# A planned kernel of attention, gated mixture and Fourier mixing: new costs for the list schedule, a new search, nine weight pairs early

## The chip, the cores and the metric

The kernel runs on one core of one Trainium2 chip. A core has five engines with instruction queues of their own: TensorE (PE) for matmuls, VectorE (DVE), ScalarE (ACT), GpSimd (POOL), and SyncE (SP), which only issues DMAs here. They meet by semaphores. The metric is the device time of one launch in microseconds (us), the median over the runs.

## The reference

Attention with a decay, whose output goes through a gated feed-forward layer with a convolution over the sequence, and then through a Fourier-mixing block. B = 4, H = 8, S = 576, D = 64, so that the hidden width is 512.

```
def _attn_ref(q, k, v, f):
    scores = scale * np.matmul(q, k.transpose(0, 1, 3, 2))
    cum = np.cumsum(np.log(np.clip(f, 0.0001, 1.0)), axis=-1)
    decay = cum[:, :, :, None] - cum[:, :, None, :]
    scores = np.where(causal, -1000000000.0, scores + decay)
    scores = scores - np.max(scores, axis=-1, keepdims=True)
    attn = np.exp(scores)
    attn = attn / (np.sum(attn, axis=-1, keepdims=True) + 1e-09)
    return np.matmul(attn, v)

def _moe_ref(x, w_in, conv_w, w_out):              # widths 512, 1024, 512
    h = np.maximum(x @ w_in, 0.0)
    conv_out = sum of conv_w[k] * (h shifted by k - 1), k = 0..2
    return h * sigmoid(conv_out) @ w_out

def _moe2_ref(x, w_ch1, w_ch2):                    # widths 512, 2048, 512
    u = x + real(fft(fft(x, axis=1), axis=2))
    un = (u - mean(u)) / sqrt(var(u) + 1e-06)
    return u + np.maximum(un @ w_ch1, 0.0) @ w_ch2
```

## The kernel before

The whole program is first recorded, then ordered by a planner, then emitted. Every call on an engine (`V.` for DVE, `A.` for ACT, `G.` for POOL, matmuls and transposes for PE, `dma` for SP) makes an operation with a cost from `cost_of`; `analyse` finds which operation must wait for which through the tiles that they touch; `graph` adds to each such pair a time lag from the table `LAG`, by the two engines. `forward` is a list schedule: it lets each engine take, of the operations that are ready by then, the one of least priority number, and charges its cost; it knows a clock of PE that halves a matmul's speed when the last tick had too little PE work, and a lock between DVE and POOL. `backward` runs the same from the end and gives new priorities, `ROUNDS` times over. Then each operation's priority is moved by a letter of the long string `SHIFT`, one letter for each operation, from -32 to +31 us, and a last `forward` gives the order in which everything is emitted:

```
    def order(self):
        self.graph()
        prio = [o.prio for o in self.ops]
        for _ in range(ROUNDS):
            self.forward(prio)
            prio = self.backward()
        for i, c in enumerate("".join(SHIFT.split())):
            prio[i] += 1e3 * (LETTERS.index(c) - 32)
        self.span, out = self.forward(prio)
        return out
```

On the chip the engines run that order, each in its own row, and wait by semaphores; the planner's times are not used. Since one helper emits all operations, the line in the trace is L601 for nearly all of them (L593 for groups of matmuls, L599 for fills); the names of the tiles tell what an instruction is. In the order of the changed kernel these lines are L604, L596 and L602, and the buffer numbers of the names differ by a few (psatt_u__166 for psatt_u__169).

The stages, as far as they are needed:

- **Attention**, 16 pairs of heads (0 to some 250 us). A pair's scores come as 16 and then 8 products into four PSUM tiles `psatt_s`, from `att_qk` (one buffer for the odd pairs, 70, one for the even, 91). DVE reduces each tile into `att_t` and a running minimum `att_nb` (the trace's CUSTOM_DVE_ANT_0, the order's ISA), ACT takes the exponential. The weights are then transposed on PE, 128 x 128 at a time and in groups of three or four, into two PSUM tiles `psatt_u`, and evacuated into `att_pt`: of a pair's eight groups the first two by DVE (512 wide), the next two half by ACT and half by DVE (256 each), the rest by ACT (512 and 384). These groups run about two pairs behind the scores. Then follow the products with the values (`att_tv`), also into `psatt_u`, and two multiplications on DVE into `att_xr`.
- **First feed-forward layer**, beside it and up to some 450 us with the Fourier transform (`psdft`): products into two PSUM tiles `psbc_bc`, `glu_t` and `glu_cv` for the convolution and the gate, with SCALAR_TENSOR_TENSOR of 576 on DVE and TENSOR_TENSOR of 576 on POOL.
- **Fourier block's two products** w_ch1 and w_ch2, 450 us to the end, dense on PE.
- **Weights** come as 64-bit floats and are decoded, 512 columns at a time, in the buffers `wprep_dr` (raw), `wprep_dw`, `wprep_de`: an ACT Abs (ACTIVATE `wprep_dw<-wprep_dr`), a POOL clamp (TENSOR_SCALAR), on DVE a TENSOR_SCALAR and two SCALAR_TENSOR_TENSOR. The tiles of w_out are also folded (a sum of 255 columns on POOL, a difference of 255 on DVE, an ACT copy `wprep_dr<-wprep_de`). `NST` pairs of tiles (one of w_ch1, one of w_ch2) of the 16 are decoded in the attention stage and stored in DRAM; the others late, by `decode_some`.

The functions that the change touches, and their callers:

## Time and profile before

| | |
|---|---|
| median of 3 runs | 857.21 us (856.75 to 858.38) |
| the profiled execution | 855.14 us, its span 853.4 us |
| PE busy | 821.7 us, 96% |
| DVE busy | 651.7 us, 76% |
| ACT busy | 432.8 us, 51% |
| POOL busy | 250.1 us, 29% |
| granted clock of PE, mean | 0.994 |

The span runs from the first to the last instruction; 1.7 us of the execution lie outside it. A row of the timeline gives an instruction's start, its length, its engine, what it writes and reads, and in brackets how long the engine had been idle before it and what it waited for. A matmul's row is longer than the time to the next one's start, since matmuls overlap; the starts tell the pace. The clock is given as a share of 2.4 GHz: 1.00, or 0.50 for 1.2 GHz.

### The profile page before, as it was taken

What the parts mean: (1) busy time and instruction counts of PE and PEld (TensorE: products, weight loads), DVE (VectorE), ACT (ScalarE), POOL (GpSimd) and SP (SyncE); (2) the same over time, 40 slices, a digit from 0 to 9 for tenths busy, and PEclk for the clock granted to TensorE, in tenths of its full rate; (3) what the DMA queues carried; (4) which work ended last, traced back from release to release, by engine and by line L of the source; (5) the groups of instructions that cost most, each with busy time, mean ns of one, the idle gap of its engine ahead of it and who ended that gap; (6) DMA issues with size and microseconds to landing.
All of it is one profiled execution on the core that took longest, in us unless ns stands there. A gap on an engine that the chain in (4) does not pass through costs nothing.

```text
span 853.4 us, 15323 instructions
## 1 busy us (share of the span) xinstructions
PE 821.7 (96%) x5424; PEld 710.6 (83%) x5424; DVE 651.7 (76%) x1596; ACT 432.8 (51%) x1043; POOL 250.1 (29%) x271
## 2 busy tenths in 40 slices
PE   8989998999999999999999999999999999999997
PEld 6657876789888998998888788888889889888896
DVE  6969998875996484269598869879877799867754
ACT  6968887854875384256435344335424453213220
POOL 2244445500451142148747441122113220000000
PEclk9989999999999999999999999999999999999999
DMA  6555464888338634686998744543552835332312
GB/s 225 156 167 176 142 208 133 262 271 269 106 123 283 196 114 145 206 250 175 261 249 199 166 132 99 186 124 101 180 175 82 214 102 154 94 124 63 99 51 86
DMA packets 97804, 139.61 MB, mean 164 GB/s; under 512 B 17048, under 2 KB 59832, under 8 KB 97728
## 3 DMA queue, kind: packets, MB, share of 16 engines
q1 hardware_dynamic: 97152, 135.69, 53.6%
q0 software_dynamic: 576, 2.95, 1.1%
q8 instruction: 42, 0.69, 0.3%
q14 instruction: 34, 0.28, 0.1%
HBM read 105.99 MB, written 35.04 MB: 165 GB/s over the span
## 4 chain that ended last, share of the span: by engine, by line
PE 70%; DVE 13%; ACT 8%; POOL 4%; issue 3%; DMA 2%; SPq 0%; DVEq 0%; ACTq 0%; POOLq 0%
PE psc_c__4743 L601 10%; PE psc_c__4742 L601 10%; PE psbc_bc__554 L601 8%; PE psbc_bc__555 L601 7%; PE psdft_x__3934 L601 5%; PE psdft_x__3935 L601 4%; PE psc_c__5054 L601 4%; PE psc_c__5053 L601 4%; PE psc_c__5051 L601 3%; PE psc_c__5052 L601 3%; PE psatt_u__174 L593 2%; DVE glu_cv__158 L601 2%; DVE glu_cv__157 L601 2%; PE psatt_s__170 L593 2%; PE psatt_u__174 L601 2%
## 5 line engine op out<-in xcount | busy, mean ns | idle before, releaser
L601 ACT ACTIVATE bc_xs__131<-ml_t__5380 128x320 fp32r<-128x320 f32 (+1 forms) x78 | 34.9, 449 | 99.6 <-DVE ml_t__5380 L601 86.6
L601 PE MATMUL psbc_bc__554<-bc_xs__131,bc_wi__130 128*128 128x288 f32 x384 | 68.3, 304 | 2.7 <-ACT glu_t__138 L601 2.2
L601 PE MATMUL psbc_bc__555<-bc_xs__131,bc_wi__130 128*128 128x288 f32 x384 | 67.2, 304 | 0.3 <-ACT glu_t__139 L601 0.3
L601 PEld LDWEIGHTS psbc_bc__554<-bc_xs__131,bc_wi__130 128*128 128x128 f32 x384 | 55.6, 189 | 5.1 <-ACT glu_t__138 L601 2.9
L601 DVE TENSOR_TENSOR ml_t__5380<-psc_c__4742,ml_t__5380 128x320 f32<-128x320 f32 (+1 forms) x91 | 40.8, 459 | 23.5 <-PE psc_c__4742 L601 22.1
L601 PEld LDWEIGHTS psbc_bc__555<-bc_xs__131,bc_wi__130 128*128 128x128 f32 x384 | 55.7, 190 | 1.2 <-ACT glu_t__139 L601 0.5
L601 DVE TENSOR_TENSOR ml_t__5380<-psc_c__4743,ml_t__5380 128x320 f32<-128x320 f32 (+1 forms) x91 | 40.6, 459 | 15.9 <-PE psc_c__4743 L601 14.0
L601 POOL TENSOR_SCALAR wprep_dw__125<-wprep_dw__125 128x512 f32<-128x512 f32 x24 | 18.5, 771 | 114.6 <-ACT wprep_dw__125 L601 114.6
L601 DVE SCALAR_TENSOR_TENSOR bc_xs__131<-ml_t__5380,bc_xs__131 128x320 fp32r<-128x320 f32 (+1 forms) x78 | 38.3, 495 | 11.8 <-ACT bc_xs__131 L601 11.0
L601 DVE SCALAR_TENSOR_TENSOR glu_cv__157<-glu_t__138,bc_cw__132,glu_cv__157 128x576 f32<-128x576 f32 x32 | 32.3, 1009 | 11.2 <-ACT glu_cv__157 L601 10.9
L601 DVE SCALAR_TENSOR_TENSOR glu_cv__158<-glu_t__139,bc_cw__132,glu_cv__158 128x576 f32<-128x576 f32 x32 | 32.6, 1018 | 4.6 <-ACT glu_cv__158 L601 4.3
L601 POOL TENSOR_SCALAR wprep_dw__122<-wprep_dw__122 128x512 f32<-128x512 f32 x24 | 17.9, 746 | 56.6 <-ACT wprep_dw__122 L601 56.6
L601 ACT ACTIVATE ml_t__5382<-ml_t__5380 128x320 fp32r<-128x320 f32 (+1 forms) x26 | 11.7, 449 | 37.9 <-DVE ml_t__5380 L601 37.6
L593 PE MATMUL psatt_s__171<-att_t__67,att_t__66 64*128 64x288 f32 (+2 forms) x48 | 25.4, 530 | 0.0
L593 PE MATMUL psatt_s__170<-att_t__67,att_t__66 64*128 64x288 f32 (+2 forms) x48 | 25.4, 529 | 0.0
L601 DVE COPY glu_t__140<-psbc_bc__555 128x256 f32<-128x256 f32 (+2 forms) x48 | 10.0, 258 | 19.5 <-PE psbc_bc__555 L601 19.5
L593 PE MATMUL psatt_u__174<-att_pt__101,att_tv__92 128*64 128x448 f32 (+3 forms) x80 | 24.0, 452 | 0.4 <-ACT att_pt__102 L601 0.4
L593 PE MATMUL psatt_u__174<-att_pt__102,att_tv__93 128*64 128x448 f32 (+3 forms) x80 | 24.0, 452 | 0.0
L601 ACT ACTIVATE glu_t__140<-psbc_bc__554 128x256 f32<-128x256 f32 (+2 forms) x48 | 8.6, 249 | 25.8 <-PE psbc_bc__554 L601 16.6
L593 PE MATMUL psatt_s__173<-att_t__67,att_t__66 64*128 64x288 f32 (+2 forms) x48 | 20.9, 442 | 0.0
L593 PE MATMUL psatt_s__172<-att_t__67,att_t__66 64*128 64x288 f32 (+2 forms) x48 | 20.8, 439 | 0.0
L593 PE MATMUL psatt_u__169<-att_pt__101,att_tv__99 128*64 128x448 f32 (+4 forms) x72 | 19.3, 413 | 1.2 <-ACT att_pt__102 L601 1.2
(895 smaller groups left out, 2984.5 us busy)
## 6 DMA issues: line engine op xcount, KB each, us to landing
wprep_dr__124<-in_moe_w_ch_dram SPq DMA_DIRECT2D x16, 512.0 KB
wprep_dr__121<-in_moe_w_ch_dram SPq DMA_DIRECT2D x16, 512.0 KB
bc_wo__133<-dram_t__334 SPq DMA_DIRECT2D x13, 512.0 KB
bc_wo__134<-dram_t__334 SPq DMA_DIRECT2D x13, 512.0 KB
att_qk__70<-in_qk_dram SPq DMA_DIRECT2D x8, 608.0 KB
att_qk__91<-in_qk_dram SPq DMA_DIRECT2D x8, 608.0 KB
att_rb__68<-dram_t__333 SPq DMA_DIRECT2D x32, 144.0 KB
dram_t__340<-mr_us__4770 SPq DMA_DIRECT2D x18, 256.0 KB
```

Of the source, the lines that this page charges most:

```text
L593: getattr(eng[op.eng], f)(**{k: v.real() if isinstance(v, View) else v for k, v in kw.items()})
L601: getattr(eng[op.eng], op.fn)(**kw)
```

## The change

Six edits, and all of them act on the order alone, except the first:

- `NST` is 9 instead of 8: one more pair of tiles of w_ch1 and w_ch2 is decoded and stored in the attention stage (34 decodes of 512 there, 32 before; 14 late instead of 16). The number of instructions on each engine and their shapes stay the same.
- `ROUNDS` 17 instead of 53, and a new string `SHIFT` with a new letter for nearly every operation.
- `LAG`: from ACT and DVE to PE 160 and 135 ns instead of 275 and 250, and other, smaller changes.
- `cost_of`: new costs of transposes, Abs, scans, DVE's transposes and POOL's operations; the fixed surcharge for DVE operations within SBUF goes.
- The lock: an operation of DVE (four kinds without PSUM) and one of POOL (two kinds) now delay each other both ways, by what is left of the other one less 90 ns. Before, only DVE paid, 0.8 of the rest of a POOL `tensor_tensor`.
- PE counts as slow when the tick before held under 2500 of work, 3060 before.

```diff
-NWO, NST = 2, 8
+NWO, NST = 2, 9
...
-ROUNDS = 53
+ROUNDS = 17
...
-BSSSSzeZSZ89LigeKBR0aZhwnRmwGp--4-+6++mq-s06+-F-8-6u-alusvgW+66w8ulcpbqmiXV+RBCsuVT+UXRzudhlCz99-BsL23wSPSJBIX
+zKThh1797sjlR+1-h3lY-7e37-pBVDcR9K0--w4ttttowXB0sv7BU0rjUYPCNZSRoYPDmfRXSTDB98-fZiBB3XUwhs--bBBBDBvdBBqjGYuaBQ
...
-       "ACT": {"ACT": 153.0, "DVE": 152.0, "PE": 275.0, "POOL": 170.0, "SP": 135.0},
-       "DVE": {"ACT": 128.0, "DVE": 127.0, "PE": 250.0, "POOL": 155.0, "SP": 120.0},
-       "POOL": {"ACT": 75.0, "DVE": 75.0, "PE": 300.0, "POOL": 102.0, "SP": 67.0},
+       "ACT": {"ACT": 153.0, "DVE": 152.0, "PE": 160.0, "POOL": 190.0, "SP": 135.0},
+       "DVE": {"ACT": 120.0, "DVE": 127.0, "PE": 135.0, "POOL": 190.0, "SP": 120.0},
+       "POOL": {"ACT": 110.0, "DVE": 115.0, "PE": 300.0, "POOL": 102.0, "SP": 105.0},
...
-        return (n * 2 if fn == "transpose" else n * 4 if kw["rhs"].dtype == F32 else max(n, 256)) / 2.4 + 12.0
+        if fn == "transpose":
+            return n * 2 / 2.4 + 2.0
+        if kw["rhs"].dtype == F32:
+            return n * 4 / 2.4 + 12.0
+        return max(n, 256) / 2.4 + (12.0 if n < 400 else 15.0)
...
-        if n > 32 and fn != "memset" and not psum and space.get("out") != "PSUM":
-            c = 1.25 * c + 60.0
         return c
     if fn == "tensor_scalar":
-        return n * 0.833 + 244.0
+        return n * 0.91 + 148.0
...
-def two_reads(fn, kw):
-
-    v = [x for x in kw.values() if isinstance(x, View)]
-    if fn in ("memset", "reciprocal") or "PSUM" in [x.t.slot.pool.space for x in v]:
+def two_reads(eng, fn, kw):
+
+    if eng == "POOL":
+        return fn in ("tensor_tensor", "tensor_scalar")
+    if eng != "DVE" or fn not in ("tensor_tensor", "scalar_tensor_tensor", "tensor_scalar", "tensor_copy"):
         return False
-    return max(x.free() for x in v) > 32
+    return "PSUM" not in [x.t.slot.pool.space for x in kw.values() if isinstance(x, View)]
...
-                if busy.get(tick - 1, 0) < 3060:
+                if busy.get(tick - 1, 0) < 2500:
...
-            if o.eng == "POOL" and o.fn == "tensor_tensor":
-                port.append((t, t + o.took))
-            elif o.pair:
-                o.took = (o.cost - 60.0) / 1.25
-                for a, b in port[-8:]:
-                    if a <= t < b:
-                        o.took += (b - t) * 0.8
-                        break
+            if o.pair:
+                k = o.eng == "POOL"
+                o.took += max(port[1 - k] - 90.0 - t, 0.0)
+                port[k] = t + o.took
```

What this does to the order, at three places. The first is DVE's row at the start, where the first pair's scores are reduced. Before:

```order
L601 SCALAR_TENSOR_TENSOR att_t_0__67<-att_rb__68,att_t_0__67 32x576 x2
L601 TENSOR_SCALAR wprep_de__126<-wprep_dw__125 128x512
L601 ISA att_t_0__75,att_nb__95<-psatt_s__170,att_t_0__65 128x288
L601 ISA att_nb__95 128x1
L601 ISA att_t_0__72,att_nb__95<-psatt_s__170,att_t_0__65 128x192
```

And now:

```order
L604 SCALAR_TENSOR_TENSOR att_t_0__67<-att_rb__68,att_t_0__67 32x576 x2
L604 ISA att_t_0__75,att_nb__95<-psatt_s__167,att_t_0__65 128x288
...
L604 ISA att_t_0__71,att_nb__95<-psatt_s__169,att_t_0__65 128x64
L604 ISA att_nb__95 128x1
L604 ISA att_t_0__76,att_nb__96<-psatt_s__170,att_t_0__65 128x64
L604 ISA att_nb__96 128x1
L604 TENSOR_SCALAR wprep_de__126<-wprep_dw__125 128x512
```

The decode's first step on DVE went from ahead of the eight reduces to behind them.

The second is ACT's row where the eighth pair's weights are evacuated (`att_pt`) and a w_out tile is prepared (`wprep_dr__121<-wprep_de__123`). Before:

```order
L601 ACTIVATE att_pt_0__101<-psatt_u__174 128x2x128
L601 ACTIVATE att_pt_0__102<-psatt_u__169 128x2x128
L601 ACTIVATE bc_xs__131<-att_xr__69 128x576
L601 ACTIVATE wprep_dr__121<-wprep_de__123 128x4x128
L601 ACTIVATE att_pt_0__101<-psatt_u__174 128x4x128
L601 ACTIVATE att_t_0__87,att_sum__103<-att_t_0__87,att_nb__105 128x192
L601 ACTIVATE att_pt_0__102<-psatt_u__169 128x4x128
```

And now:

```order
L604 ACTIVATE att_pt_0__101<-psatt_u__171 128x4x128
L604 ACTIVATE bc_xs__131<-att_xr__69 128x576
L604 ACTIVATE att_pt_0__102<-psatt_u__166 128x4x128
L604 ACTIVATE att_pt_0__101<-psatt_u__171 128x3x128
...
L604 ACTIVATE att_pt_0__102<-psatt_u__166 128x3x128
L604 ACTIVATE att_rt__98<-psatt_u__171 10x128
...
L604 ACTIVATE att_t_0__89,att_sum__103<-att_t_0__89,att_nb__105 128x448
L604 ACTIVATE wprep_dr__121<-wprep_de__123 128x4x128
```

The copy of the w_out tile stands behind the pair's last evacuation, where it stood ahead of four of them. A like exchange is found in the third pair: before, ACT's row has an evacuation `att_pt_0__101<-psatt_u__169 128x2x128`, the Abs `wprep_dw__122<-wprep_dr__121`, and the evacuation `att_pt_0__102<-psatt_u__174 128x2x128`; now both evacuations stand ahead of the Abs.

The third is PE's row behind the first 16 score products of the twelfth pair, where the tenth pair's weights are transposed (`psatt_u<-const`). Before:

```order
L593 MATMUL psatt_s__173<-att_t_0__67,att_t_0__66 128x64
L601 MATMUL psbc_bc__555<-glu_t_0__145,bc_wo__134 128x288
...
L601 MATMUL psatt_u__174<-const_t_0__61,att_t_0__85 128x128 x4
L601 MATMUL psbc_bc__555<-glu_t_0__145,bc_wo__134 128x288
...
L601 MATMUL psbc_bc__555<-glu_t_0__156,bc_wo__134 128x288
L601 MATMUL psatt_u__174<-const_t_0__61,att_t_0__82 128x128
L601 MATMUL psbc_bc__554<-glu_t_0__141,bc_wo__133 128x288
L601 MATMUL psatt_u__174<-const_t_0__61,att_t_0__82 128x128
```

And now:

```order
L596 MATMUL psatt_s__170<-att_t_0__67,att_t_0__66 128x64
L604 MATMUL psatt_u__171<-const_t_0__61,att_t_0__85 128x128 x4
L604 MATMUL psatt_u__166<-const_t_0__61,att_t_0__90 128x128 x4
L604 MATMUL psatt_u__171<-const_t_0__61,att_t_0__82 128x128 x2
...
L604 MATMUL psatt_u__171<-const_t_0__61,att_t_0__84 128x128 x4
L604 MATMUL psatt_u__166<-const_t_0__61,att_t_0__89 128x128 x4
L604 MATMUL psatt_u__171<-const_t_0__61,att_t_0__83 128x128 x3
L596 MATMUL psatt_s__167<-att_qk__91 128x448
```

The products of the feed-forward layer (`psbc_bc`) that stood between the groups are gone from there; 27 transposes stand in a row, with the twelfth pair's last eight score products directly behind. On DVE the order at this place is: copy of 512, a reciprocal of 10 columns, copy of 512, two reduces of 288, copy of 256, a reduce of 192, copy of 256.

At the end of the program the last four steps on DVE are the same in both orders (two additions of 256 from one PSUM bank, one of 512, two of 256 from the other bank). On PE the last three matmuls of 512 stand behind the end of the first bank before, the last ten now.

## Rows read from the trace of the kernel before

**Rows 1.** The page: busy time of each engine, share of the span, instructions.

```profile
PE 821.7 (96%) x5424; PEld 710.6 (83%) x5424; DVE 651.7 (76%) x1596; ACT 432.8 (51%) x1043; POOL 250.1 (29%) x271
```

**Rows 2.** Windows: stretch, length, busy PE, PEld, DVE, ACT, POOL (instructions), PE clock, DMA share, GB/s.

```profile
0.00:62.00 62.00, 54.04 (x368) 36.99 (x370) 47.77 (x173) 46.21 (x136) 18.60 (x40) 0.94 0.58 183
62.00:250.00 188.00, 178.20 (x1398) 150.39 (x1395) 159.96 (x413) 137.06 (x359) 74.97 (x62) 0.99 0.59 188
250.00:450.00 200.00, 192.85 (x1457) 176.35 (x1456) 131.06 (x286) 104.91 (x256) 82.92 (x84) 1.00 0.71 207
450.00:845.00 395.00, 392.73 (x2191) 344.23 (x2191) 309.72 (x721) 144.22 (x293) 73.64 (x86) 1.00 0.45 128
845.00:853.40 8.40, 3.87 (x17) 2.63 (x15) 3.16 (x7) 0.42 (x1) 0.00 (x0) 0.99 0.35 109
```

**Rows 3.** Windows around the two stretches with a lower granted clock.

```profile
51.00:54.40 3.40, 1.54 (x11) 1.15 (x11) 2.45 (x6) 2.05 (x6) 0.61 (x1) 1.00 0.23 57
54.40:61.30 6.90, 6.20 (x28) 2.80 (x28) 3.48 (x13) 5.08 (x16) 2.54 (x2) 0.51 0.36 108
143.20:146.60 3.40, 3.40 (x15) 2.98 (x15) 1.76 (x9) 3.39 (x9) 2.74 (x2) 0.50 0.41 140
```

**Rows 4.** Timeline of POOL, DVE and PE at the first scores.

```profile
10.39 0.61 POOL L601 TENSOR_SCALAR wprep_dw__125<-wprep_dw__125 128x512 f32<-128x512 f32 x1 [7.95 <-ACT wprep_dw__125 L601]
11.04 0.43 DVE L601 TENSOR_SCALAR wprep_de__126<-wprep_dw__125 128x512 int32<-128x512 int32 x1 [1.84 <-POOL wprep_dw__125 L601]
12.17 1.02 PE L593 MATMUL psatt_s__170<-att_qk__70 64*128 64x448 f32 x2 [1.22 <-DVE att_nb__95 L601]
```

**Rows 5.** Timeline of ACT, DVE and PE at the third pair's transposes.

```profile
52.06 0.66 ACT L601 ACTIVATE wprep_dw__122<-wprep_dr__121 128x512 f32<-128x512 f32 x1 [1.37 <-DMA wprep_dr__121<-in_moe_w_in_dram]
53.03 0.42 DVE L601 COPY att_pt__102<-psatt_u__174 128x256 f32<-128x256 f32 x1 [0.95 <-ACT att_pt__102 L601]
53.51 0.66 PE L601 MATMUL psatt_u__174<-const_t__61,att_t__79 128*128 128x128 f32 x4 [1.32 <-DVE att_pt__102 L601]
```

**Rows 6.** Timeline of PE, DVE and ACT at the eighth pair's transposes.

```profile
139.33 0.66 PE L601 MATMUL psatt_u__174<-const_t__61,att_t__84 128*128 128x128 f32 x4 [1.40 <-DVE att_pt__101 L601]
140.09 1.38 DVE L601 TENSOR_TENSOR wprep_de__123<-wprep_dw__125 128x255 f32<-128x255 f32 x1
141.55 0.63 ACT L601 ACTIVATE wprep_dr__121<-wprep_de__123 128x512 fp32r<-128x512 f32 x1 [3.30 <-DVE wprep_de__123 L601]
142.72 0.55 PE L601 MATMUL psatt_u__174<-const_t__61,att_t__83 128*128 128x128 f32 x3 [1.71 <-ACT att_pt__101 L601]
```

**Rows 7.** Timeline of DVE: reduces of score tiles, a decode's step, two copies.

```profile
11.38 0.45 DVE L601 CUSTOM_DVE_ANT_0 att_t__75<-psatt_s__170,att_t__65 128x288 f32<-128x288 f32 x1
...
11.75 0.35 DVE L601 CUSTOM_DVE_ANT_0 att_t__72<-psatt_s__170,att_t__65 128x192 f32<-128x192 f32 x1
...
13.85 0.69 DVE L601 SCALAR_TENSOR_TENSOR wprep_dw__125<-wprep_dr__124,wprep_de__126 128x512 int32<-128x512 int32 x1
...
133.75 0.63 DVE L601 COPY att_pt__101<-psatt_u__174 128x512 f32<-128x512 f32 x1
...
138.86 0.41 DVE L601 COPY att_pt__101<-psatt_u__174 128x256 f32<-128x256 f32 x1
```

**Rows 8.** Timeline of PE and DVE at the end.

```profile
848.02 0.85 PE L601 MATMUL psdft_x__3934<-mr_t__4769,bc_xs__131 128*128 128x512 f32 x3
848.78 0.74 DVE L601 SCALAR_TENSOR_TENSOR wprep_dw__122<-wprep_dw__122,bc_cw__132,ml_yt__5400 128x512 f32<-128x512 f32 x1
849.63 0.88 DVE L601 SCALAR_TENSOR_TENSOR wprep_dw__122<-psdft_x__3934,bc_cw__132,wprep_dw__122 128x256 f32<-128x256 f32 x2
```

**Rows 9.** Timeline of POOL and DVE: a gating step beside POOL's work, and one alone.

```profile
242.19 1.64 POOL L601 TENSOR_TENSOR bc_xs__131<-att_xr__108,bc_xs__131 128x576 fp32r<-128x576 f32 x1
242.44 2.00 DVE L601 SCALAR_TENSOR_TENSOR glu_cv__157<-glu_cv__157,glu_t__138 128x576 f32<-128x576 f32 x1
...
248.64 0.81 DVE L601 SCALAR_TENSOR_TENSOR glu_cv__158<-glu_t__139,bc_cw__132,glu_cv__158 128x576 f32<-128x576 f32 x1
```

More of the change, by code (lines that the diff above doesn't have):

```diff
@@ new lines @@
+K44BCHhfOOBEBSEJUo69HvGZ--+-HkBIySLWHJCOEBOqL0--aVBEKBfJBBLIBHGEBBBBCDCGHGBBGBLEDFQBBBBBBBSBBBBBBBBLCBBBCOrOiB
+8LgPJFBGb4cSKGa9c+-PBBDBBDDDMFDFDPKDEDDNKGJJJIFPFDSHGKcgdFDDDPDDFbOFOEIEDDHHIMt6YyZuebVUL49oUVOh+0JbPejh-yE--v
+JONcWJ+gB86QKMEBNc5nB+9fBLEOFRtZMy++++SECDDLJDUWjjaQNcNOOZKXwWfkWJLnsvYOEBhMDf0mdPRgQCyBbUrMdJUK4ML98osWDFRBLY
+ynIINRRFEd703+5P5+-FVdjix-4Ez-qSZKIFY+XD040ESYkqG8EBi64-+UCEUEMPLQbxDCCBRMRKEYUVczmrjhElBcCLsgbKEDEOoU0vPUCfRS
+sQu7n6576eQ-9mOUjoK87Vg-hj-8-9-ph997-+hP8snF5EEjxd-M--CCBCSDFCEbHEHDFCFTPfEE8zfNXwOtFCEGDGDgVC7oT8ztSSp01z2zx-
@@ new lines @@
+110w79+8---+6F-XKYnp9-+CRYms8-HfsDOEEGcMFhEmjhVRKIDO2wleIJdi+DgStXMCNEIBHDFKETEEEDBEHFFHMLPHEgFHo-dcHhHhQX-wsE
+Ftw41aGLHoQmGmOPTEhUBQSiaGP6nrmneMOKBBUYyuonjbm-KioQIMBRjDRBBBBSUSjUVYfyY57710drQMTkuPC68+0Wy+219++9---1j0177-
+-869+607SC114511865--87-051jw5n83gl50z3irYU7y87x7U5+xrmHMOvQFGPahGCRSJpnCBJOCXeCCBBCBEEBBDC7T++FDHEDJCBGT1fDGH
+BHUUOkyJEkddhflBBGGSHDKBE+CJJHDDJ-DOIfHFIGavaki7rYZeZksZQskbl613tXg+k-PBBCCOBStnKCHLLJCBFBdBCBBaDFBGHCOFFj1IBD
+GHGCBUZNmOEEC5BBiiGEFDPHkHRUTZ6rQkpPdclvWptjxtHMzwDbvTEOHBUUHTBGCtLDDtGCEIDDECSBJbLafWgdpcZgwUT42jhneV7--+gZjh
@@ L112 @@
+4p53ujut3xst95gov-74p6jWhgdhl-zh6gh-269v9uUNebuyD0eM1BEJnWWVWcaihcfbXanZZapNYWngHWQeK4qkSTKWcgjnwl8eofddt8slad
+ja8VZnkk-88wzggu-zy839v5+jrj8t8fkhqyx--2--------------u60tfhlsxu2vw50-20vwtuz9ebmsyttfjleWSuTh1cpkjZW9o5aV177d
+sR3sVWT1PzhYhIGILGZXY2-----1999----tqGVJEHHDFDJBBBJBLZRd23VBSPeXMWTeTMX2MD-rNGTCj----omtWMGIDGlQO
 """
@@ L308, in cost_of @@
         c = n * 0.833 + (51.0 if psum else 93.0) + 94.0 * ptr
-        if kw.get("func") == AF.Ln and o.p[0] == 0:
-            c += 1200.0
+        if kw.get("func") == AF.Abs:
+            c += 35.0
         return c + (93.0 if "accum_out" in kw else 0.0)
@@ L313, in cost_of @@
         c = n / 0.96 + 68.0 + 61.0 * ptr
+        if fn == "transpose":
+            return c + 30.0
         if fn in ("tensor_scalar", "tensor_copy") and not psum and space.get("out") != "PSUM":
@@ L454, in graph @@
             o.work = 0.0
-            o.pair = o.eng == "DVE" and two_reads(o.fn, o.kw)
+            o.pair = bool(o.eng) and two_reads(o.eng, o.fn, o.kw)
             if o.eng == "PE":
@@ L499, in forward @@
     def forward(self, prio):
-        ops, busy, port = self.ops, {}, []
-        wire = [0.0]
+        ops, busy = self.ops, {}
+        wire, port = [0.0], [-1e9, -1e9]
         def place(i, t):
```

127 lines of the change are left out of this document (58 added, 69 removed).

## The prediction

> **What bounds the kernel now.** I read the totals of the page first: TensorE (PE) is busy 821.7 of 853.4 us, VectorE (DVE) 651.7, ScalarE (ACT) 432.8, GpSimd (POOL) 250.1 [rows 1]. PE's work is the same in both kernels, so what can go or come is PE's idle time, 31.7 us, and the time in which it runs at the lower of its two clocks. The windows [rows 2] say where the idle time lies: 8.0 us in the first 62 (62.00 less 54.04), 9.8 up to 250 (the attention stage with the first mixture layer beside it), 7.2 up to 450, 2.3 in the 395 us after that, 4.5 in the tail. So 46% of the time, from 450 to 845, has nothing to give: PE is busy 99.4% of it. Two stretches ran at 1.2 GHz instead of 2.4: 54.4 to 61.3 with a granted clock of 0.51, 143.2 to 146.6 with 0.50 [rows 3]. The 6.20 and 3.40 us of PE work in them would have taken half, so they cost about 3.1 and 1.7 us. Both come behind idle time: PE had worked 1.54 us of the 3.40 before the first [rows 3]. All there is to win is 31.7 + 4.8 = 36.5 us, in many pieces: the largest single waits are 1 to 2 us each [rows 4 to 6].
>
> **The change part by part.** The same instructions run, in another order (the one difference in kind: two more weight tiles of w_ch1 and w_ch2 are decoded in the attention stage instead of late). The new costs, lags, lock and threshold act only through that order, so I cost the order at the places where PE waits now, against this execution.
>
> *A, the first scores.* The reduces of the first eight score tiles free the tiles that PE writes next. Ahead of them on DVE stands the first step of a weight decode, at 11.04. It waits for POOL (10.39 + 0.61), which waits for the decode's ACT Abs; PE waits 1.22 us to 12.17 [rows 4]. In the new order this step stands behind the eight reduces. PE had written all the products of the block by 10.95 (12.17 less 1.22), the first of them earlier, while the first reduce starts at 11.38 [rows 7] and PE's next block needs the first two reduces alone. If they start 1.2 us earlier, PE's whole wait goes: **1.2 us gained**. The bound below is 0, if something else of the start comes as late.
>
> *B, the third pair.* An ACT Abs that waited for a DMA until 52.06 stands ahead of an evacuation of transposed attention weights; DVE's copy at 53.03 follows, PE waits 1.32 us to 53.51 [rows 5], and the slow stretch of 3.1 us starts 0.9 us later. In the new order both evacuations stand ahead of the Abs. Up to 4.4 us go. But the new order has the pair's next eight score products directly behind fourteen transposes, and these need tiles that eight DVE reduces free; eight such reduces took from 11.38 to 13.85, 2.5 us [rows 7], of which I take half to be covered by the transposes. I take **3.1 gained** (4.4 less 1.3), bounds 0 and 4.4.
>
> *C, the tail.* The last four steps on DVE are two pairs of additions from PSUM and, between them, one addition of 512 (0.74 at 848.78) that the last pair needs. PE's last three matmuls start at 848.02 and end at 848.87 (0.85 later); the last pair starts at 849.63, since the one of 512 stands behind the first pair [rows 8]. In the new order ten matmuls (2 to 2.8 us by the 0.85 of three) run behind the end of the other bank, so the first pair and the addition of 512 are done when PE ends: 849.63 - 848.87 = 0.76, less some 0.1 for the signal: **0.65 gained**, little doubt.
>
> *D, the eighth pair's transposes.* PE waits 1.40 us at 139.33 for a DVE copy and 1.71 at 142.72 for an ACT evacuation; this one stands behind an ACT copy of folded w_out weights at 141.55, which waited 3.30 us for the fold's DVE subtraction, 1.38 us at 140.09 [rows 6]; then 3.4 us at the lower clock [rows 3]. In the new order the ACT copy of this place stands behind all seven evacuations. So 1.71 and the 1.7 of the clock go; the first wait I leave, since a DVE copy still has reduces and a gating step ahead of it: **3.4 gained**, bounds 0 and 4.8.
>
> *E, the tenth pair's transposes.* Before, 27 transposes of this pair are spread among 35 and more matmuls of the mixture layer, and PE does not wait there. In the new order all 27 stand together (2.9 us: 0.11 each by the 0.66 of four and the 0.55 of three in [rows 6]). They go through two PSUM tiles in seven groups, each to be evacuated before the group after next. DVE has two copies of 512 (0.6 each by the 0.63 of [rows 7]), two reduces (0.37 by their starts), a copy of 256 (0.41), a reduce of 192 (0.35) and another copy of 256 in a row [rows 7], 3.1 us that begin when the first group is there, at 0.44; then the sixth group starts, and the seventh behind it: 3.1 + 0.44 + 0.44 + 0.33 = 4.3 us in place of 2.9, with some 0.1 for signals on the way: **1.5 lost** at least. If a gating step ahead of these copies is held up by POOL (2.00 us at 242.44, beside POOL's 1.64 from 242.19, against 0.81 free at 248.64 [rows 9]) it is 1.2 more. I take **2.1 lost**; with a slow stretch behind it like D's, 4.4. The two gating steps show that a DVE step can take 1.2 us longer when POOL works beside it [rows 9]. The Trainium skill, "SBUF — State Buffer", section "Who interferes with whom", says that an operation of DVE with two SBUF inputs contends with a POOL operation that reads SBUF, as an exclusive lock; the rows agree. By it E would cost 2.7 whenever POOL runs there, and the sum below would be 0.6 worse.
>
> *F, the ninth pair of tiles.* Two more decodes stand in the attention stage, some 1.8 us of DVE each: 0.43 as at 11.04 [rows 4] and twice 0.69 as at 13.85 [rows 7]. DVE is busy 159.96 of 188 us between 62 and 250 [rows 2], so 3.6 us fit into 28 that are free, but not always at the right moment: bounds 0 and 3.6, I take **1.0 lost**, nearer to 0. What leaves the late stage gains nothing, as PE does not wait there.
>
> *The rest*, some 20 us of small waits, is ordered anew as well. I found in the order no reason for either sign: 0, give or take 3. Between 250 and 450 the lock shows most (POOL busy 82.92 of 200 us, PE idle 7.2 [rows 2]), and an order that prices it could gain there.
>
> The sum: -1.2 - 3.1 - 0.65 - 3.4 + 2.1 + 1.0 = -5.25 us. The profiled execution took 855.14 us, 1.7 more than its span and 2.1 less than the median of the runs, 857.21; the same step from the median gives **852.0 us**.
>
> **The rivals.**
> 1. *The lock pays too.* If the priced lock also takes half of the 7.2 us of 250 to 450, and E costs 1.5, then -5.25 - 3.6 - 0.6 = -9.5: 847.8 us. For it: DVE steps of 2.00 that take 0.81 free. Against it: in the new order the gating steps and POOL's products still come in the same numbers beside each other.
> 2. *The stalls only move.* DVE is the second engine (85% in 62 to 250), and the new order takes nothing from its work in the attention stage and adds F's. If B, D and E come to zero together, A, C and F remain: -0.85, 856.4 us, no change that a measurement tells.
> 3. *More time at the lower clock*, the one that ends slower. Each stretch behind a wait costs 1.7 to 3.1 us here [rows 3]. If B and D lose none of theirs since other waits of 1 us come at these places, and E brings one of 1.7, then A and C (-1.85) stand against E's 2.7 + 1.7 and F's 1.0: +3.55, 860.8 us; with E alone at 2.1 it is 860.2 or, with F at nothing, 859.2. It decides from the point at which the new order has more than the 10.3 us at half rate that the old one has. For it: the 27 transposes in a row. Against it: the single waits that precede both stretches are those that the new order resolves. The Trainium skill, "TensorE: Matmul & The Clock Gate", section "A second HAM failure mode: psum-queue depth-cycling", tells of the same: short idle times between groups of matmuls that cycle through PSUM tiles make the clock swing between its levels. By that rule the time would be this rival's; the trace bears it out at two places, and elsewhere not: idle time of 7.2 us between 250 and 450 left the granted clock at 1.00 [rows 2].
> 4. *The change does nothing to the order*: excluded, since the two orders differ from the eleventh instruction of DVE on.
>
> **How the numbers follow.** Chances: the forecast, 848 to 855.4, 0.47; rival 1, 0.13; rival 2, 0.18; rival 3, 0.22. A measurement of this kernel tells some 0.2% from no change, that is 1.7 us: below 855.5 is faster, above 858.9 slower. Faster: 0.47 + 0.13 = 0.60; same 0.18; slower 0.22. The range reaches down over most of rival 1 (all gains at their upper bound, E at 1.5 and F at 0: -1.2 - 4.4 - 0.7 - 4.8 + 1.5 = -9.6, and 2 of the lock, 845.6) and up to rival 3: 845.5 to 860.5.
>
> **What would show it.** A: PE's first wait for a reduce gone and the second block of scores at about 11 instead of 12.17. B and D: the granted clock at 1.0 in the stretches that answer to 51 to 62 and 138 to 147, and no PE wait above 1 us there. C: DVE's last pair starting within 0.2 us of PE's end. E: a wait of 1.5 to 2.7 us for copies of transposed weights at about 165 us, the only larger one that is new. The prediction is wrong if the clock shows more than two stretches at 0.5, if PE's idle time up to 250 us stays at 17.8, or if the 395 dense us of the late stage become longer.

## The result, and the profile after

The changed kernel takes 847.43 us (median of 4 runs, 847.37 to 849.06), the kernel before in the same comparison 856.98 (855.99 to 858.38): a ratio of 0.9892, 95% interval 0.9874 to 0.991, or 9.55 us less. The forecast was 852.0 in a range of 845.5 to 860.5, so sign and range held, and the gain is 4.3 us larger than the sum. The reasons held less well than the number, as the runs below show.

The page of the changed kernel (its profiled execution took 847.47 us), then its windows, with the columns of [rows 2]:

```profile
span 845.7 us, 15316 instructions
PE 821.6 (97%) x5424; PEld 707.1 (84%) x5424; DVE 638.1 (75%) x1596; ACT 431.9 (51%) x1043; POOL 244.8 (29%) x271
```

```profile
0.00:62.00 62.00, 55.92 (x406) 39.07 (x406) 51.17 (x184) 49.25 (x145) 16.50 (x39) 1.00 0.60 191
62.00:250.00 188.00, 182.43 (x1444) 153.03 (x1443) 157.30 (x431) 140.34 (x379) 75.36 (x65) 1.00 0.61 193
250.00:450.00 200.00, 192.70 (x1430) 177.13 (x1430) 134.26 (x280) 103.28 (x238) 90.00 (x96) 1.00 0.76 216
450.00:838.00 388.00, 386.67 (x2134) 334.99 (x2132) 292.53 (x698) 139.00 (x283) 62.94 (x73) 1.00 0.42 122
```

Against [rows 2], PE's busy time up to 250 us rises from 232.24 to 238.35, with more matmuls done (1850 in place of 1766), and the granted clock is 1.00 in every stretch: in this execution the two stretches of [rows 3] are gone. In the other three executions the clock was 0.995 or 0.996 on average over the span, which is some 7 to 8 us at half rate (in the profiled one it is 1.7 us, all behind PE's last matmul), and they took 847.37, 847.39 and 849.06 us. The kernel before, in the 61 executions timed with the experiments, was granted 0.990 to 0.997; the 12 of them at 0.995 or 0.996 took 854.8 us on average. So at like clocks some 7 of the 9.55 us remain, and the clock is the smaller part of the gain. From 250 to 450 PE is as busy as before (192.70, before 192.85), and behind that it has next to no idle time in either kernel. So the gain of the changed kernel is made in the first 250 us. Attention lasts longer than that, other than the list of stages has it: its last matmul starts at 355.6 us in the kernel before and at 341.7 now.

To see where, I laid each trace beside that of before by the matmul work that PE had done (each matmul counted at the duration that its form has at full clock) and took the difference of the two times at equal work. The table has the lead over the kernel before in us, at the time that the kernel before has there; the last rows are kernels of the experiments:

```
time of before    26.5  49.4  79.1  99.2 133.6 149.4 176.5 267.4 277.5 363.8 493.6 848.9
changed kernel     2.1   0.0   4.7   3.4   7.6  12.9  10.0  11.3  10.6   7.0   8.2   6.9
b_abcd             0.0   0.0   3.1   3.1   3.0   5.2   2.9   2.8   2.8   2.8   1.1   1.8
h75                2.3   0.3   4.9   2.5   2.4   2.3   2.4   2.3   2.3   2.3  -0.7  -0.3
h250               2.8  -0.7   4.0   2.7   6.9  12.1   9.3  10.8   1.9   1.9   2.0   2.6
n_before           0.4  -0.4   2.7   2.2   2.0   7.0   6.5   8.6   7.6   7.0   1.2   4.6
n_after            2.8   1.2   2.9   1.4   4.9  10.5   7.0  10.8  10.6   6.5   5.8   9.6
```

The profiled execution of before was a good one (855.14, its median is 856.98), so the last column is some 1.8 us short of what the medians say for the changed kernel. Single executions differ: b_abcd, h75 and h250 have the order of before between 364 and 494 us, and there they lose 1.7 us, lose 3.0 and gain 0.1. The changed kernel gains 4.7 us at 49 to 79 (part B's place), 4.2 at 99 to 134, 5.3 at 134 to 149 (part D's), loses 2.9 behind that (part E's), and 3.6 more between 278 and 364.

Where the orders differ most, between 79 and 330 us, the entries also depend on how matmuls that overlap are counted. With each counted at the whole length of its row, or only at what its row adds to the one before, the gain at 99 to 134 comes out at 4.4 or 3.1 in place of 4.2, the loss at E's place at 1.7 or 4.0 in place of 2.9, and the loss between 278 and 364 at 5.9 or 2.8 in place of 3.6. The changed kernel's entries at 49, 149, 364 us and behind move by at most 0.7.

### The profile page after: what moved, and what is told of

The parts are those of the page before. It is cut to its first block, busy times and chain, and to the rows that moved or that the text cites. A ratio compares the mean times of both kernels' runs of the same rounds, so it can differ in the third digit from the quotient of the medians.

```text
span 845.7 us, 15316 instructions
## 1 busy us (share of the span) xinstructions
PE 821.6 (97%) x5424; PEld 707.1 (84%) x5424; DVE 638.1 (75%) x1596; ACT 431.9 (51%) x1043; POOL 244.8 (29%) x271
## 4 chain that ended last, share of the span: by engine, by line
PE 79%; DVE 8%; DMA 5%; ACT 3%; issue 2%; POOL 2%; SPq 0%; DVEq 0%; ACTq 0%; POOLq 0%
PE psc_c__4803 L604 10%; PE psc_c__4802 L604 10%; PE psbc_bc__547 L604 9%; PE psbc_bc__546 L604 9%; PE psdft_x__3942 L604 5%; PE psdft_x__3943 L604 5%; PE psc_c__5049 L604 4%; PE psc_c__5050 L604 4%; PE psc_c__5048 L604 4%; PE psc_c__5047 L604 4%; PE psatt_u__166 L604 3%; PE psatt_s__167 L596 3%; PE psatt_u__171 L596 3%; PE psatt_u__171 L604 3%; PE psatt_u__166 L596 2%; PE psatt_s__169 L596 2%
## 5 line engine op out<-in xcount | busy, mean ns | idle before, releaser
L604 PE MATMUL psbc_bc__547<-bc_xs__131,bc_wi__130 128*128 128x288 f32 x384 | 65.4, 301 | 0.8 <-ACT glu_t__139 L604 0.8
L604 PE MATMUL psbc_bc__546<-bc_xs__131,bc_wi__130 128*128 128x288 f32 x384 | 66.1, 303 | 0.0
L604 PEld LDWEIGHTS psbc_bc__547<-bc_xs__131,bc_wi__130 128*128 128x128 f32 x384 | 54.9, 188 | 1.6 <-ACT glu_t__139 L604 1.0
L604 PEld LDWEIGHTS psbc_bc__546<-bc_xs__131,bc_wi__130 128*128 128x128 f32 x384 | 54.3, 188 | 1.5 <-issue 0.5
L604 POOL TENSOR_SCALAR wprep_dw__125<-wprep_dw__125 128x512 f32<-128x512 f32 x24 | 16.3, 681 | 117.0 <-ACT wprep_dw__125 L604 117.0
L604 DVE SCALAR_TENSOR_TENSOR bc_xs__131<-ml_t__5395,bc_xs__131 128x320 fp32r<-128x320 f32 (+1 forms) x78 | 36.2, 470 | 10.4 <-ACT bc_xs__131 L604 9.2
L604 POOL TENSOR_SCALAR wprep_dw__122<-wprep_dw__122 128x512 f32<-128x512 f32 x24 | 16.3, 679 | 79.0 <-ACT wprep_dw__122 L604 79.0
L604 ACT ACTIVATE wprep_dw__125<-wprep_dr__124 128x512 f32<-128x512 f32 x24 | 16.0, 667 | 12.6 <-DMA dram_t__347<-wprep_dw__125 5.5
L596 PE MATMUL psatt_u__171<-att_pt__101,att_tv__92 128*64 128x448 f32 (+3 forms) x80 | 21.6, 417 | 0.3 <-ACT att_pt__102 L604 0.3
L596 PE MATMUL psatt_u__171<-att_pt__102,att_tv__93 128*64 128x448 f32 (+3 forms) x80 | 21.6, 417 | 0.0
```

The costliest lines, as they stand in the source:

```text
L596: getattr(eng[op.eng], f)(**{k: v.real() if isinstance(v, View) else v for k, v in kw.items()})
L604: getattr(eng[op.eng], op.fn)(**kw)
```

## The experiments

Every operation has a number in the recorded program, and the planner ends with a list of these numbers. The first eight kernels move single operations in that list, each together with those in between that depend on it, and change nothing else. My theory was that of the prediction: single waits, and the half-clock stretch behind each, are what the new order removes. Its rival was the prediction's second, that stalls only move.

### Parts A, B and D alone, and together with C

```diff
+MOVES = [(61, 105, True)]                       (b_a: decode step behind eight reduces)
+MOVES = [(132, 388, True)]                      (b_b: ACT Abs behind two evacuations)
+MOVES = [(479, 1467, True)]                     (b_d: ACT copy behind seven evacuations)
...
         self.span, out = self.forward(prio)
+        for i, j, late in MOVES:
+            out = self.move(out, i, j, late)
         return out
```

b_abcd has all three and (7567, 7555, False): the addition of 512 ahead of the first pair.

> The kernel before, with one step of its order moved: the first DVE step of the weight decode that stands ahead of the first eight score reduces goes behind them (part A of the prediction alone). By the prediction's term the wait of 1.22 us at 12.17 goes and the kernel is 1.2 us faster (0.9986). The rival: DVE has no free time between 11 and 30 us, so the step is only done later there, PE waits for it or for what stands behind it at 26 to 30 us, and the time does not change (1.000).

> The kernel before, with the ACT Abs of a weight decode moved behind the two evacuations of the third pair's transposes (part B alone). If what counts here is the single wait and the half-clock stretch behind it, PE's wait of 1.32 us at 53.51 goes, the clock from 54 to 61 is 1.00 and the kernel is 4.4 us faster (0.9949). The rival, the stalls only move: the Abs comes later, another wait of about 1 us comes at 55 to 75 us, the clock falls all the same, and the time changes by less than 1 us.

> The kernel before, with the ACT copy of a folded w_out tile moved behind the seven evacuations of the eighth pair's transposes (part D alone). If the single wait and the stretch behind it count, PE's wait of 1.71 us at 142.72 goes with the 3.4 us at half clock: 3.4 us faster (0.9960), up to 4.8 if the wait of 1.40 goes too. The rival, the stalls only move: the fold's copy comes later, its weights are late for the next mixture products, and the time changes by less than 1 us.

> The kernel before, with four steps of its order moved: those of A, B and D, and in the tail the addition of 512 ahead of the first pair (part C). If the gain of the change is the sum of a few waits at these places, this has nearly all of it without the new durations, lock or threshold: 1.2 + 4.4 + 3.4 + 0.65 = 9.65 us faster by the terms (0.9887, the ratio that the changed kernel has); 8.4 if A is given back. If the gain comes from the newly ordered program as a whole (the rest that the prediction put at 0, the priced lock), these four moves give under half of it, less than 4.8 us (above 0.9944).

| kernel | median us | of before | 95% interval |
|---|---|---|---|
| b_a | 856.23 | 0.9995 | 0.9979 to 1.0011 |
| b_b | 854.57 | 0.9991 | 0.9975 to 1.0006 |
| b_d | 856.33 | 1.0017 | 1.0002 to 1.0032 |
| b_abcd | 854.36 | 0.9977 | 0.996 to 0.9994 |

My theory fell. None of the three is faster by itself (b_d is, if anything, slower), and all four moves give 2.0 us by the ratio, 1.3 by the medians, where 8.4 to 9.65 were expected. The traces show how the stalls move. In b_a the wait of 1.22 us [rows 4] is gone, and others stand there (timeline of PE; the bracket has the idle time ahead of the instruction and what ended it):

```profile
14.66 0.51 PE L612 MATMUL psatt_s__170<-att_qk__91 64*128 64x288 f32 x1 [0.62 <-DVE att_nb__95 L620]
...
17.72 0.64 PE L612 MATMUL psatt_s__170<-att_qk__91 64*128 64x448 f32 x1 [0.27 <-DVE att_nb__104 L620]
...
19.75 0.28 PE L620 MATMUL psatt_u__174<-const_t__61,att_r__97 128*10 128x128 f32 x1 [0.54 <-DVE att_r__97 L620]
```

In b_b the copy of DVE and the evacuation of ACT do come ahead of the Abs, but the Abs then holds up the next evacuations. In place of the waits of 1.32 [rows 5] and 0.34 (at 54.86) stand 0.28 and 0.71; the 0.67 ahead of them was there before. And the clock falls all the same, for 3.4 us in place of 6.9 (timeline of PE, then a window):

```profile
51.47 0.66 PE L620 MATMUL psatt_u__169<-const_t__61,att_t__74 128*128 128x128 f32 x4 [0.67 <-DVE att_pt__101 L620]
...
52.41 0.66 PE L620 MATMUL psatt_u__174<-const_t__61,att_t__79 128*128 128x128 f32 x4 [0.28 <-DVE att_pt__102 L620]
...
53.77 0.55 PE L620 MATMUL psatt_u__169<-const_t__61,att_t__73 128*128 128x128 f32 x3 [0.71 <-ACT att_pt__101 L620]
```

```profile
56.00:58.00 2.00, 2.00 (x8) 0.68 (x8) 1.54 (x9) 1.65 (x5) 0.72 (x1) 0.50 0.04 11
```

In b_d the half-clock stretch of [rows 3] at 143 is gone (granted clock 1.00 from 136 to 150), and yet the kernel is no faster: the wait of 1.71 became 1.11, and two waits stand 12 to 18 us later, of which the kernel before had only the second, at 0.90:

```profile
142.47 0.55 PE L620 MATMUL psatt_u__169<-const_t__61,att_t__88 128*128 128x128 f32 x3 [1.11 <-ACT att_pt__102 L620]
...
155.15 0.44 PE L620 MATMUL psatt_u__174<-const_t__61,att_t__77 128*128 128x128 f32 x2 [0.94 <-DVE att_pt__102 L620]
...
160.97 0.55 PE L620 MATMUL psatt_u__174<-const_t__61,att_t__78 128*128 128x128 f32 x3 [1.31 <-ACT att_pt__102 L620]
```

Nor are the half-clock stretches the whole price of the old order. The profiled execution of b_abcd has none, and over its ten executions the granted clock is 0.998 on average, where the kernel before has 0.9935; it is still only 2.0 us faster (window over its whole span):

```profile
0.00:851.30 851.30, 817.62 (x5424) 708.57 (x5424) 653.26 (x1596) 433.42 (x1043) 248.06 (x271) 1.00 0.55 164
```

### The same on the changed kernel: its three largest waits relieved

```diff
+MOVES = [(920, 1900, True), (1894, 2128, False), (1900, 2127, False),      (a_e)
+         (2136, 1990, True), (2139, 1990, True), (2140, 1990, True)]
+MOVES = [(4103, 3721, True)]                                               (a_lock)
+MOVES = [(54, 274, True), (225, 296, False), (274, 296, False)]            (a_s)
```

a_els has all of them.

> The changed kernel, with the tenth pair's transposes relieved (part E): on DVE the gating step goes behind the copies of transposed weights, the copies go ahead of the two reduces, and on ACT three exps go behind the last evacuation. In the changed kernel the 27 transposes last 4.87 us in place of 2.9 and PE waits 0.35, 0.43 and 1.06 us for their copies. If E is a price of this order, the waits go and it is 2 to 3 us faster than the changed kernel (about 844.9 us, 0.986 of the kernel before). The rival: the reduces and the gating step are then late for the scores and mixture products behind them, PE waits as long there, and the time stays within 0.8 us of the changed kernel's 847.4.

> The changed kernel, with the DVE subtraction of one 128x512 weight tile (3.61 us at 410.15 beside four POOL operations, 0.65 to 0.69 where POOL is idle) moved behind the DFT steps that it holds up. If the lock of that one place costs what PE waits behind it, 1.97 us at 415.40, it is 2.0 us faster than the changed kernel (845.4, 0.9865). The rival: the weights come late for the products that want them, or the next DVE step with two SBUF inputs is held up in its place, and the time does not change (0.9892).

> The changed kernel, with three steps of DVE's start moved: one decode step that POOL holds up (1.26 us at 26.24 for 128x10) goes later, a reciprocal and a 64-wide reduce go earlier. PE waits 1.95 us for them at 28.30, which gives back the 1.2 us of part A. If it is the order that gives them back, this is 1.5 to 2 us faster than the changed kernel (845.7, 0.987). The rival: DVE has no free time from 11 to 30 us, and PE waits as long elsewhere before 35 us: no change (0.9892).

> The changed kernel with all three sets of moves (tenth pair, the subtraction beside POOL, the start). If the three waits are independent prices, 5 to 6.5 us faster than the changed kernel: 841 to 842.5 us (0.982). If the stalls only move, within 1 us of the changed kernel.

Of the kernel before, they are 0.9921 (0.99 to 0.9942), 0.9892 (0.9867 to 0.9918), 0.9895 (0.9867 to 0.9923) and 0.9922 (0.99 to 0.9943), in the order of the list; the changed kernel is 0.9892. Three hoped-for gains of 2 us each came to nothing, and the two kernels with a_e's moves are 2.2 us slower than the changed kernel by the medians, though their intervals overlap with its own. The clearest is a_s. It has no wait at 28 us any more and is 2.0 us ahead of the changed kernel from 32 to 320 us of PE work. Most of the lead goes between 350 and 362 us, at a transfer: a_s issues the last load of `dft_t__3765` ahead of this wait at 352.55, 2.0 us before the changed kernel does (354.56), but PE can go on only 0.7 us earlier (timeline of PE in a_s, then in the changed kernel):

```profile
349.81 0.54 PE L625 MATMUL psbc_bc__546<-glu_t__145,bc_wo__134 128*128 128x288 f32 x2 [1.62 <-DMA bc_wo__134<-dram_t__336]
...
361.62 0.47 PE L625 MATMUL psdft_x__3949<-dft_t__3765,dft_t__3767 128*128 128x512 f32 x1 [1.90 <-DMA dft_t__3765<-dram_t__375]
```

```profile
351.74 0.53 PE L604 MATMUL psbc_bc__546<-glu_t__145,bc_wo__134 128*128 128x288 f32 x2 [1.30 <-DMA bc_wo__134<-dram_t__336]
...
362.29 0.47 PE L604 MATMUL psdft_x__3949<-dft_t__3765,dft_t__3767 128*128 128x512 f32 x1 [0.65 <-DMA dft_t__3765<-dram_t__375]
```

a_s starts the first of these 1.9 us earlier than the changed kernel and the second only 0.7. It loses the rest at 416 to 420 us, at half clock behind a wait of 1.93 us; the changed kernel has that wait too, 1.97 at 415.40, and its clock stayed at 1.00. In a_e the waits of 0.43 and 1.06 us became 0.27 and 0.58, and one for an ACT evacuation of 2.30 us stands between them. In a_els the same wait of 2.30 us was followed by a half-clock stretch; a_e, with the same wait, had none (granted clock 1.00 from 158 to 176 us). Row and window of a_els:

```profile
161.79 0.55 PE L632 MATMUL psatt_u__171<-const_t__61,att_t__83 128*128 128x128 f32 x3 [2.30 <-ACT att_pt__101 L632]
```

```profile
163.00:170.00 7.00, 6.42 (x32) 3.31 (x30) 3.18 (x11) 5.57 (x20) 0.00 (x0) 0.53 0.62 203
```

a_lock says little: the wait of 1.97 us is gone, and the moved subtraction is still held up, 2.25 us at 413.34; but its profiled execution waited 3.08 us for the transfer of `bc_wo__134` at 352.8 (1.30 in the changed kernel, though the two orders do not differ up to there), so that such a wait varies by more than what was to be measured.

### A stretch of the new order in the old one

So I formed another theory: not a place, but the order of a whole stretch makes the gain. Two kernels are the kernel before with the first 533 or 2186 operations in the changed kernel's order:

```diff
         self.span, out = self.forward(prio)
-        return out
+        head = the list of the changed kernel's first operations
+        done = set(head)
+        return head + [i for i in out if i not in done]
```

> The kernel before, whose first 533 operations (up to some 75 us) stand in the changed kernel's order, the other 7039 in their old order. The four moves of A to D gave 0.2% in place of the 1.1% hoped for, so single places do not explain the gain. Theory now: the order of a whole stretch does, and the gain comes in two such stretches. By the lead of the changed kernel at equal TensorE work (4.1 to 4.7 us at 75 us) this is some 4.4 us faster than before (0.9949). Rival: what is gained up to 75 us is lost again at the next stall, as with the single moves: under 1 us (above 0.9988).

> The kernel before, whose first 2186 operations (up to some 250 us, the attention stage) stand in the changed kernel's order, the other 5386 in their old order, the ninth pair of weight tiles late as before. If the gain is made in the attention stage and kept, this has all of it: the lead at 250 us is 10.6 us (0.9876), less up to 2.7 that the changed kernel gives back at 310 to 390 us. Rival: a lead is lost at the weights' transfers at 340 to 400 us, which come by their own time, or the old order behind the cut does not fit: under 5 us (above 0.994).

h75 measured 0.9967 (0.9952 to 0.9982), 2.5 us less; h250 0.9971 (0.9955 to 0.9987), 2.8 us less. By the medians h75 lies between its two expectations, and h250 is where its rival was (under 5 us, since the old order behind the cut does not fit). By the traces, one execution each, the theory held up to the joint: h250 follows the changed kernel's lead to 10.8 us at 267 (table above), with 4.7 and 5.2 us at the places of B and D, as there. Then one wait takes most of it. The old order has the load of a weight tile, which the new one issues at 255.60, on SP behind the store of a decoded tile, and it goes out 7.7 us later (timeline of SP's queue and PE in h250; in the changed kernel):

```profile
262.90 0.32 SPq L671 DMA_DIRECT2D dram_t__355<-wprep_dw__125  x1
263.32 0.38 SPq L671 DMA_DIRECT2D bc_wo__133<-dram_t__336  x1
...
267.94 0.58 PE L671 MATMUL psbc_bc__546<-glu_t__141,bc_wo__133 128*128 128x288 f32 x1 [7.04 <-DMA bc_wo__133<-dram_t__336]
```

```profile
255.60 0.45 SPq L604 DMA_DIRECT2D bc_wo__133<-dram_t__336  x1
```

h75 loses 2.4 us of its 4.9 at its own joint and keeps the rest to 364 us. So the order of the first 250 us is worth some 11 us at 267 us in these traces, and an order is good only with the one that follows.

### Without the search

The change gives the planner a better model and a new string of searched shifts. The last two kernels keep each model and set all shifts to zero (the letter g):

```diff
-BSSSSzeZSZ89LigeKBR0aZhwnRmwGp--4-+6++mq-s06+-F-8-6u-alusvgW+66w8ulcpbqmiXV+RBCsuVT+UXRzudhlCz99-BsL23wSPSJBIX
...
+gggggggggggggggggggggggggggggggggggggggggggggggggggggggggggggggggggggggggggggggggggggggggggggggggggggggggggggg
...
```

> The kernel before with every searched shift of its priorities at zero, so that its old durations and its one-way lock alone set the order. With n_after it tells what the new durations, lags, two-way lock and threshold are worth by themselves, without the search. If the better model gives the gain, n_after is faster than this by 5 us or more; if the search gives it, the two are alike within some 3 us. Both are slower than the searched kernels: by 10 to 40 us, since the pieces of idle time that a search removes are some 1 us each.

> The changed kernel with every searched shift of its priorities at zero: the new durations, lags, two-way lock and threshold alone set the order. If the better model gives the gain, it is 5 us or more faster than the same of the kernel before; if the search on it gives the gain, the two are alike within some 3 us, or this is the slower one.

| kernel | median us (lowest to highest) | of before | 95% interval |
|---|---|---|---|
| before | 856.17 (852.29 to 859.39) | 1 | |
| n_before: old model, no shifts | 850.07 (848.84 to 850.82) | 0.9928 | 0.9913 to 0.9942 |
| n_after: new model, no shifts | 846.23 (844.82 to 847.42) | 0.9882 | 0.9865 to 0.9899 |
| changed: new model, new shifts | 847.43 (847.37 to 849.06) | 0.9892 | 0.9874 to 0.991 |

The last row is from the first comparison, with the ratio to its own runs of the kernel before.

I had expected the kernels without shifts to be 10 to 40 us slower. They are faster. The old model's order without its searched shifts is 6.1 us faster than with them; the new model takes 3.8 us more, which lies between the two marks that I had set (5 and 3); the new search adds nothing that can be measured (the intervals of the last two rows overlap). So nearly two thirds of the change's gain is the loss of the old string. And the clock is not what n_before gains by: it was granted 0.994 on average over its six executions, as much as the kernel before.

Where n_before gains is less clear. In its one trace the lead grows at the places of B and D, 3.1 us from 49 to 79 and 5.0 from 134 to 149 (3.4 to 5.3 by the other ways to count). But of 7.0 us at 364 only 1.2 are left at 494, behind half-clock stretches at 404 and 466, and 3.4 of the 4.6 at the end are gained after that; n_after gains 3.8 there, and the changed kernel loses 1.3. So the dense late stage has something to give after all, though PE is busy in it: from 494 us to the last matmul n_before does nearly the same number of matmuls in 4.6 us less, of which 1.0 is idle time of PE. Why its matmuls follow each other faster, no run shows (windows of the kernel before, then of n_before):

```profile
494.00:848.80 354.80, 352.85 (x1973) 310.76 (x1972) 275.24 (x652) 125.10 (x259) 47.66 (x51) 1.00 0.42 121
```

```profile
494.00:844.20 350.20, 349.28 (x1968) 310.72 (x1966) 268.40 (x650) 125.44 (x258) 46.66 (x51) 1.00 0.42 123
```

At B's place the windows of 50 to 62 us, in the kernel before, n_before and the changed kernel, show the difference:

```profile
50.00:62.00 12.00, 9.31 (x48) 4.83 (x48) 7.37 (x24) 7.51 (x22) 3.15 (x3) 0.72 0.39 122
```

```profile
50.00:62.00 12.00, 9.66 (x73) 6.32 (x71) 9.54 (x29) 9.25 (x26) 4.72 (x5) 1.00 0.30 97
```

```profile
50.00:62.00 12.00, 10.53 (x85) 7.02 (x85) 10.29 (x35) 11.18 (x33) 4.49 (x5) 1.00 0.53 173
```

The same 12 us hold 48, 73 and 85 matmuls. n_before waits there too, for 0.67, 0.69, 0.36 and 0.62 us, much like b_b, but its clock stays up there (it fell at 12 to 16, 404 to 408 and 466 to 470 us instead).

What the old string did shows in the planner's own times of these orders (`span` of its last `forward`, worked out from the kernels without the chip). The old model puts its order at 831.64 us without the string and at 824.52 with it: the search took 7.1 us off the model's time and added 6.1 to the chip's, so what it found was in the model and not on the chip. The new model has 829.78 without its string and 827.33 with it.

Three things stay open. The two models differ in durations, lags, lock, threshold, the number of backward rounds and the ninth pair, and which of these gives the 3.8 us was not tried. Neither string was tried on the other model. And which errors of the old model its string made use of was not shown.

## Why the prediction was right or wrong, point by point

**What bounds it** held in part. PE's idle time up to 250 us fell from 17.8 to 11.65, and the late stage gave nothing in the changed kernel (386.67 of 388 us busy; before 392.73 of 395). But that a stage in which PE is busy has nothing to give is refuted by n_before and n_after, which gained 3.4 and 3.8 us behind 494. And of the four executions only the profiled one is without half-clock stretches.

**A** (1.2 forecast): the wait itself went, and the second block of scores starts at 11.34 in place of 12.17. The step that failed is that nothing else of the start comes as late, my lower bound of 0. The changed kernel is 2.1 us ahead at 26 us and has lost it by 49: PE waits 1.95 us for what stands behind a step on ten columns that POOL's product holds up.

```profile
11.34 1.02 PE L596 MATMUL psatt_s__167<-att_qk__70 64*128 64x448 f32 x2
...
26.20 1.26 POOL L604 TENSOR_TENSOR bc_wi__130<-wprep_dw__125,bc_wi__130 128x512 fp32r<-128x512 f32 x1 [11.34 <-ACT bc_wi__130 L604]
...
26.24 1.26 DVE L604 TENSOR_SCALAR att_r__106<-att_sum__103 128x10 f32<-128x10 f32 x1
...
28.30 0.27 PE L604 MATMUL psatt_u__166<-const_t__61,att_r__106 128*10 128x128 f32 x1 [1.95 <-DVE att_r__106 L604]
```

**B** (3.1, upper bound 4.4) measured 4.7 and **D** (3.4, upper bound 4.8) 5.3, both above their bounds. Both waits of D went, B's 1.32 became 0.85, and neither half-clock stretch is there in this execution. But the step behind the numbers was wrong: I named one operation at each place as the cause, and b_b and b_d, which move that operation alone, gain nothing that can be measured. h250, with the order of the whole stretch, has 4.7 and 5.2 at these places, so it takes an order of the stretch and not one operation; I had read one wait of a chain as if it were the only one. How much of it is the clock, single executions cannot tell: b_abcd, without a half-clock stretch, has 3.1 at B's place.

```profile
51.72 0.65 PE L604 MATMUL psatt_u__171<-const_t__61,att_t__79 128*128 128x128 f32 x4 [0.85 <-DVE att_pt__102 L604]
```

**C** (0.65) held. The last pair on DVE starts at 841.97, when PE ends at 841.93 (841.09 and 0.84); before it was 0.76 late [rows 8]. So this signal took 0.04 us, where I had allowed 0.1 without a row to show it.

```profile
841.09 0.84 PE L604 MATMUL psdft_x__3942<-mr_t__4835,bc_xs__131 128*128 128x512 f32 x3
841.97 0.88 DVE L604 SCALAR_TENSOR_TENSOR wprep_dw__122<-psdft_x__3942,bc_cw__132,wprep_dw__122 128x256 f32<-128x256 f32 x2 [0.77 <-PE psdft_x__3942 L604]
```

**E** (a loss of 2.1, bounds 1.5 and 4.4) measured 2.9 at its place. The mechanism was that of the prediction in part: reduces stand ahead of the copies, and PE waits for the copies (0.35 us at 157.59, 0.43 at 159.35). The gating step, 0.81 alone [rows 9], was held up beside POOL and took 1.51, but it cost the copies nothing: it ended at 156.57, and DVE then waited for PE until its first copy at 156.84. The largest wait is one that I had not counted, 1.06 us for an ACT evacuation. No half-clock stretch followed.

```profile
155.06 1.51 DVE L604 SCALAR_TENSOR_TENSOR glu_cv__158<-glu_cv__158,glu_t__139 128x576 f32<-128x576 f32 x1 [0.46 <-ACT glu_cv__158 L604]
...
156.84 0.69 DVE L604 COPY att_pt__101<-psatt_u__171 128x512 f32<-128x512 f32 x1 [0.28 <-PE psatt_u__171 L604]
...
159.35 0.66 PE L604 MATMUL psatt_u__171<-const_t__61,att_t__84 128*128 128x128 f32 x4 [0.43 <-DVE att_pt__101 L604]
...
164.67 0.59 PE L596 MATMUL psatt_u__166<-att_pt__101,att_tv__99 128*64 128x448 f32 x1 [1.06 <-ACT att_pt__102 L604]
```

**F** (1.0) is not seen: the ninth pair is decoded at 287 to 298 us, later than I had taken (attention goes on to 341.7), and between 222 and 331 us PE has no wait above 0.31.

**The rest** (0, give or take 3) is the term that was most wrong: 4.2 us gained at 99 to 134, where waits of 0.27 to 0.69 us of the kernel before went (1.8 us in all; where the rest comes from is not shown), and 3.6 lost at 278 to 364. Of the 10.0 us at 176 us, B, D and E make 7.1.

So the time fell into the range partly by luck: A and F came to nothing, B and D went over their bounds for another reason than the one given, and the rest brought gains and losses that no term had. And what n_before shows to be the larger part of the change, a string of shifts that cost 6.1 us, stood in no term at all.

**The rivals.** The second, that stalls only move, lost as a forecast and won as a rule for single edits: of eight moves of one to ten steps, one (b_abcd) is faster than its base, by 2.0 us of 9.65. The first named 847.8 but for the wrong reason: the stretch from 250 to 450, where the lock was to pay, gave nothing. The third, more half-clock time, did not come: 10.3 us at half rate before, none in the profiled execution after and some 7 to 8 us in the other three. The Trainium skill, "TensorE: Matmul & The Clock Gate", section "A second HAM failure mode: psum-queue depth-cycling", tells of a kernel that cycles through PSUM banks and whose short idle times between groups of matmuls made the clock swing. By that, the 27 transposes in a row could have swung it here; in the profiled execution of the changed kernel they did not (granted clock 1.00), nor in that of a_e, but in a_els, with the same wait of 2.30 us among them as a_e, the clock fell (0.53).

## What to carry to other kernels

The wait that a trace shows may be one of several that stand close behind each other: before a gain is counted for removing one, move that one step alone and measure. A searched order should now and then be run against the same planner without the search, since here a string of 7,577 letters, which looked 7.1 us better to the planner, had cost 6 us. And a lead gained early is kept only if the transfers that it runs into come earlier by as much: waits for them took back 1.2 of 1.9 us in a_s and 8.9 of 10.8 in h250.
